# Three double banks in turn, one-hot products on GpSimd, and index arithmetic in single steps, in a kernel of attention and expert layers

## The chip, the cores and the metric

The kernel runs on one core of one Trainium2 chip. The metric is the time of one execution on the device in microseconds (us), lower is better; the median of several runs is quoted. Every experiment was timed in alternating rounds with the kernel before on the same chip. Experiments sent together share one chip, and the results number it (6, 9, 11 or 15); the chip of the first comparison was not recorded. Each number below names its chip.

Engines in the profiles: PE is the matmul engine (PEld its weight loads), DVE the vector engine, ACT the scalar engine, POOL is GpSimd (which here also issues nearly all transfers), SP issues the stores of the attention rows. "L526" is line 526 of the kernel; lines after the change are numbered 8 to 22 higher than the same lines before. A half-clock stretch is a stretch in which the recorded PE clock was 0.5.

## The reference

```python
# attention: q, k, v are (8 batches, 8 heads, 576 tokens, 64), k and v are averaged over groups of 8 tokens (72 left)
scores = (1/8) * q @ k_p^T ;  attn = softmax(scores) ;  o = attn @ v_p
x = o as 4608 tokens x 512
# expert layer: each token goes through the two layers of one of 8 experts (domain_id)
for e in range(8):
    mask = domain_id == e
    out[mask] = relu(x[mask] @ w1[e]) @ w2[e]      # w1: 512 x 1024, w2: 1024 x 512
```

## The kernel before

The work is a list of units with times in "slots", sorted and then issued in that order. The batches are taken in four pairs (pair 0 to 3). A slot is one score unit (two matmuls, then the exponential on ACT); 16 slots make a pair. Between them stand the mixing units (`av_unit`: eight matmuls, then reciprocal and product on DVE into `x_sb`), the pooling of keys and values, and the transposes of q. The rows of a token's expert are found by one-hot matmuls (`perm_*`) and some chains of short DVE operations. Rows are stored to `x_lin` in DRAM, gathered back by expert, transposed, and sent through the two expert layers. For experts 0 and 1, the first three blocks of rows come from pairs 0 to 2 alone ("early"); the other two ("late") need pair 3.

On-chip accumulator memory (PSUM) is shared by tags: `big` has two double banks, `wide` one double bank, `small` two single banks.

```python
turns = {"pre": ("big", "big", "wide"), "out": ("small", "small", "wide")}
def rot(kind):                       # rot2() takes from "pre", rot1() from "out"
    i = count_[kind]; count_[kind] = i + 1
    tag = turns[kind][i % 3]
    return {"big": big, "wide": wide, "small": small}[tag]()
# ... cut ...
def val(i):                          # product of the one-hots; two per pair
    nc.vector.tensor_tensor(box["vc"][:, i], box["eq"][:], thl[...].to_broadcast(...), op=ALU.mult)
# ... cut ...
def sc_unit(pr, bh):
    p = big()
    # two matmuls, then ACT: exp -> at
def av_unit(pr, cc):
    pv = wide() if pr < NP - 1 or cc < 4 else rot2()...
    # eight matmuls, DVE: reciprocal, then x_sb = pv * rcp; every third unit stores x_sb to x_lin
# ... cut ...
for i, (k0, k1) in enumerate(((2.0, 3.8), (4.0, 5.8), (6.0, 8.0), (18.0, 25.0))):
    put(perm_units(i), k0, k1)
    put([lambda i=i: perm_mm(i)], k1 + 0.7, k1 + 0.7)
put([perm_finish], 40.0, 40.0)       # 9 DVE steps in one block
put([orig_finish], 43.0, 43.0)       # 9 DVE steps
put([count], 46.0, 46.0)             # 12 DVE steps and a matmul
# ... cut ...
put([lambda i=i: run(turn_units_(0, i)) for i in range(2)], 62.0, 64.0)   # transposes, expert 0, early
put([lambda i=i: e0_unit(i) for i in range(8)], 64.2, 71.4)               # first layer, expert 0, early
run([x[2] for x in sorted(plan)])
# after the plan: the rest of experts 0 and 1
for e in range(2):
    for j in range(3, NBL):
        gather(e, j)                 # the late rows: wait for pair 3's stores
run(wload_units(2, 0, 1))            # 1 MB: first-layer weights of expert 2
run(merge(l2_units(0, 0, EARLY, e0["hT"]), turn_units(1, 0, 3)))
run(l1_units(1, 0, EARLY, he, 0))
run(wload_units(2, 1, 1))            # 1 MB: second-layer weights of expert 2
run(turn_units(0, 3, NBL))           # transposes of expert 0's late rows
# ... late parts of experts 0 and 1, gathers and transposes of expert 2, then experts 2 to 7 in one loop
```

The softmax here doesn't subtract the row's maximum and nothing guards it: scores larger than these inputs give would overflow.

## Time and profile before

| | |
|---|---|
| timed runs, first comparison | 274.4 us (273.3 to 275.0, 4 runs) |
| the profiled execution | 265.7 us (span 263.7 us) |

The profiled execution is 9 us shorter than the timed runs.

From the page of the kernel before: the span in 40 equal slices of 6.6 us, the busy share of PE in tenths, PE's clock and the busy share of the transfer engines.

```profile
PE   1785998998966867998889999999999999999990
...
PEclk9999599999995775799999999999999999999999
DMA  6999999999999934955994999989979969922022
```

The last row holds digits near 9 up to slice 14 (0 to 92 us): transfers run full through the attention. From slice 22 on PE holds 9: the experts are bound by matmuls. Between lies the part that can be shortened, slices 3 to 21.

The same execution by windows. Columns: window, its length, busy us (count) of PE, PEld, DVE, ACT, POOL, then PE's clock, the share of the transfer engines, GB/s.

```profile
70.00:80.00 10.00, 6.92 (x97) 4.81 (x95) 9.23 (x37) 5.25 (x8) 0.00 (x0) 0.92 1.03 244
80.00:90.00 10.00, 8.09 (x91) 5.62 (x92) 4.77 (x12) 4.99 (x9) 0.00 (x0) 0.56 1.16 245
90.00:100.00 10.00, 6.20 (x79) 3.99 (x76) 3.97 (x10) 6.71 (x13) 2.96 (x3) 0.78 0.54 163
100.00:110.00 10.00, 8.60 (x76) 5.41 (x75) 4.96 (x12) 2.12 (x4) 4.13 (x5) 0.54 0.66 121
110.00:120.00 10.00, 9.11 (x57) 4.93 (x56) 2.87 (x5) 3.05 (x6) 2.49 (x3) 1.00 0.61 147
130.00:140.00 10.00, 9.13 (x72) 6.51 (x70) 3.81 (x8) 2.74 (x7) 6.54 (x7) 1.00 1.11 281
```

From 70 to 80 us DVE is full (9.23 of 10) and PE is not (6.92). Then the clock is 0.54 to 0.78 for 30 us. What PE waited for, in total, times, longest:

```profile
PE wide L504 <- DVE x_sb L510: 5.0, 8, 0.7
PE turn L576 <- DMA xg<-x_lin,xrow: 2.2, 2, 1.3
PE small L364 <- DVE vc L352: 2.0, 1, 2.0
...
PE small L269 <- DVE nov L267: 1.1, 1, 1.1
...
PE big L597 <- DMA xg<-x_lin,xrow: 0.9, 1, 0.9
```

`x_sb` is the release of the single mixing bank; PE waited 5.0 us itself, and its weight loads 7.4 us. `vc` is the product of the one-hots, `nov` belongs to the count.

### The profile page before, as it was taken

Reading aid. Unit: us, or ns where it says so; the run is one execution under the profiler, and the core shown is the slowest. Engines: PE = TensorE matmul, PEld = TensorE weight load, DVE = VectorE, ACT = ScalarE, POOL = GpSimd, SP = SyncE. Lnnn points to the kernel's source line nnn. Section 1 sums busy time; section 2 is a strip of 40 time slices with the busy share of each in tenths; the row PEclk is TensorE's granted clock in tenths of the full one; section 3 lists DMA queues with packets and bytes.
Section 4 is the critical chain, followed back from the end, with each engine's and each line's share of the span. In section 5 each row is a group of like instructions: output and inputs, shape, how many; then the busy total and the mean of one; then the engine's idle time right before and its main releaser. Section 6 shows DMA issues by size and latency. Waiting matters only on the chain.

```text
span 263.7 us, 4980 instructions
## 1 busy us (share of the span) xinstructions
PE 230.8 (88%) x2048; PEld 148.1 (56%) x2048; DVE 124.4 (47%) x284; ACT 93.4 (35%) x157; POOL 101.3 (38%) x116
## 2 busy tenths in 40 slices
PE   1785998998966867998889999999999999999990
PEld 0664666676643644555566665665755755756640
DVE  7257788786785353524234334334234332343320
ACT  1045547877654671422132220230411312302210
POOL 7000000300000037027764775656655665734042
PEclk9999599999995775799999999999999999999999
DMA  6999999999999934955994999989979969922022
GB/s 113 207 218 218 210 221 224 239 240 241 247 243 245 241 106 157 140 145 107 243 236 162 165 237 250 221 240 205 240 187 204 259 122 211 268 109 98 2 101 92
DMA packets 18153, 50.19 MB, mean 190 GB/s; under 512 B 2316, under 2 KB 10574, under 8 KB 15568
## 3 DMA queue, kind: packets, MB, share of 16 engines
q0 software_dynamic: 16320, 45.10, 78.8%
q1 hardware_dynamic: 1808, 4.76, 4.9%
q8 instruction: 16, 0.26, 0.4%
q14 instruction: 9, 0.07, 0.1%
HBM read 67.15 MB, written 15.20 MB: 312 GB/s over the span
## 4 chain that ended last, share of the span: by engine, by line
PE 56%; DVE 14%; DMA 10%; issue 10%; POOL 4%; ACT 3%; POOLq 1%; DVEq 0%
PE big L597 13%; PE small L613 10%; PE wide L597 6%; PE wide L613 5%; DMA x_lin<-x_sb 4%; DMA out_dram<-y,tok 4%; POOL out_dram L622 4%; PE big L484 4%; DVE x_sb L510 3%; PE wide L504 3%; PE small L442 3%; PE small L413 3%; PE small L470 2%; DMA xg<-x_lin,xrow 2%; PE turn L576 2%
## 5 line engine op out<-in xcount | busy, mean ns | idle before, releaser
L562 POOL DMA_INDIRECT xg<-x_lin,xrow x40 | 40.6, 1016 | 72.3 <-DVE x_sb L510 45.3
L622 POOL DMA_INDIRECT out_dram<-y,tok x40 | 40.1, 1003 | 44.4 <-ACT y L620 20.7
L487 ACT ACTIVATE at<-big 72x576 f16<-72x576 f32 x64 | 40.2, 644 | 30.6 <-PE big L484 29.3
L613 PEld LDWEIGHTS <-hT 128*128 128x128 f16 x272 | 25.8, 98 | 26.7
L597 PEld LDWEIGHTS <-w 128*128 128x128 f16 x256 | 25.1, 100 | 13.9 <-issue 2.3
L603 DVE TENSOR_SCALAR hT<-big 128x640 f16<-128x640 f32 (+1 forms) x22 | 15.7, 716 | 33.1 <-PE big L597 33.1
L597 PE MATMUL big<-xT,w 128*128 128x320 f16 (+2 forms) x176 | 29.4, 312 | 1.8 <-DMA xg<-x_lin,xrow 0.9
L620 ACT ACTIVATE y<-small 128x512 f32<-128x512 f32 x14 | 8.4, 597 | 45.0 <-PE small L613 42.1
L601 ACT ACTIVATE hT<-big 128x640 f16<-128x640 f32 (+1 forms) x21 | 13.2, 627 | 29.0 <-PE big L597 29.0
L510 DVE TENSOR_TENSOR x_sb<-wide,rcp 128x512 f16<-128x512 f32 x33 | 22.8, 692 | 1.1
L484 PE MATMUL big<-qT,kpT 64*72 64x288 f16 x128 | 21.3, 338 | 2.0 <-DVE qT L474 1.9
L504 PE MATMUL wide<-vp,at 72*128 72x65 f16 (+1 forms) x288 | 16.8, 208 | 5.4 <-DVE x_sb L510 5.0
L577 DVE COPY xT<-turn 128x1024 f16<-128x1024 f16 (+1 forms) x24 | 14.3, 598 | 14.9 <-PE turn L576 14.9
L504 PEld LDWEIGHTS <-at 72*128 72x128 f16 (+1 forms) x320 | 14.7, 112 | 11.5 <-DVE x_sb L510 7.4
L613 PE MATMUL small<-w,hT 128*128 128x512 f16 x80 | 18.7, 379 | 0.0
L618 DVE COPY y<-small 128x512 f32<-128x512 f32 x13 | 9.0, 692 | 20.5 <-PE small L613 19.6
L576 PE MATMUL turn<-ident,xg 128*128 128x128 f16 x160 | 13.7, 226 | 2.2 <-DMA xg<-x_lin,xrow 2.2
L576 PEld LDWEIGHTS <-xg 128*128 128x128 f16 x160 | 11.1, 100 | 7.9 <-DMA xg<-x_lin,xrow 3.0
L597 PEld LDWEIGHTS <-k 128*128 128x128 f16 x128 | 12.5, 98 | 5.2
L508 DVE RECIPROCAL rcp<-wide 128x8 f32<-128x8 f32 x33 | 6.8, 205 | 16.3 <-PE wide L504 16.1
L597 PE MATMUL wide<-xT,w 128*128 128x320 f16 (+2 forms) x80 | 13.3, 299 | 0.8 <-DVE xT L577 0.8
L603 DVE TENSOR_SCALAR hT<-wide 128x640 f16<-128x640 f32 (+1 forms) x10 | 7.5, 745 | 13.3 <-PE wide L597 10.1
(158 smaller groups left out, 321.1 us busy)
## 6 DMA issues: line engine op xcount, KB each, us to landing
w<-in_moe_w_dram POOLq DMA_DIRECT2D x8, 1024.0 KB, 11.8
k<-in_k_dram POOLq DMA_DIRECT2D x4, 1152.0 KB, 27.9
q<-in_q_dram POOLq DMA_DIRECT2D x4, 1152.0 KB, 28.1
v<-in_v_dram POOLq DMA_DIRECT2D x4, 1152.0 KB, 25.3
x_lin<-x_sb SPq DMA_DIRECT2D x12, 384.0 KB, 10.3
k<-in_moe_w_dram POOLq DMA_DIRECT2D x3, 1024.0 KB, 8.5
v<-in_moe_w_dram POOLq DMA_DIRECT2D x3, 1024.0 KB, 11.0
q<-in_moe_w_dram POOLq DMA_DIRECT2D x2, 1024.0 KB, 11.2
```

The source lines that it names most:

```text
L484: nc.tensor.matmul(p[0:72, par, 0:288], s["kpT"][64 * par:64 * par + 64, bh, :], s["qT"][64 * par:64 * par + 64, :, 8 * bh:8 * bh + 8], st ...
L487: nc.scalar.activation(at[0:72, bh % 8, :].rearrange("p (a c) -> p a c", a=2), p[0:72, :, 0:288], AFT.Exp, scale=1.0 / 64.0)
L504: nc.tensor.matmul(pv[r0:r0 + z - a, h, 0:65], s["at", bt][0:72, h, a:z], s["vp"][0:72, 8 * bt + h, :], start=True, stop=True, skip_group_ ...
L510: nc.vector.tensor_tensor(out=x_sb.rearrange("p (b h a) -> p b h a", b=4, h=H), in0=pv[:, :, 0:64].rearrange("p h (a b) -> p b h a", b=4), ...
L562: i = nc.gpsimd.indirect_dma_start(out=xg[e % 2][:, j, :], out_offset=None, in_=x_lin[0:rows, :], in_offset=bass.IndirectOffsetOnAxis(ap=x ...
L576: nc.tensor.transpose(p[:, j - a, kk, :], xg[e % 2][:, j, 128 * kk:128 * kk + 128], ident[:])
L577: nc.vector.tensor_copy(xts[e][:, :, 128 * a:128 * z].rearrange("p k (j c) -> p j k c", c=128), p[:, 0:z - a])
L597: nc.tensor.matmul(p[:, a, 0:m], w1[:, kk, 128 * fi:128 * fi + 128], xT[:, kk, s0 + m * a:s0 + m * a + m], start=(kk == 0), stop=(kk == 3))
L601: nc.scalar.activation(dst, p[:, 0:nh, 0:m], AFT.Relu)
L603: nc.vector.tensor_scalar(out=dst, in0=p[:, 0:nh, 0:m], scalar1=0.0, scalar2=None, op0=ALU.max)
L613: nc.tensor.matmul(p, hT[:, fi, 128 * j:128 * j + 128], w2[:, fi, :], start=(fi == 0), stop=(fi == 7))
L622: i = nc.gpsimd.indirect_dma_start(out=out, out_offset=bass.IndirectOffsetOnAxis(ap=orig[0][:, bl:bl + 1], axis=0), in_=y[:], in_offset=No ...
```

## The change

The intent is to keep PE busy and warm from 20 to 110 us: scores and mixing rotate over three double banks instead of having two and one; the products go to idle GpSimd; the three DVE blocks are cut into single steps spread over slots 34 to 58, and the count moves behind the attention; pair 3's value pooling and the early expert work start 2 to 3 slots earlier; one 1 MB weight load goes behind the first gathers; the first expert units are reordered. The operations and their number are the same but for a few.

```diff
-                nc.vector.tensor_tensor(box["vc"][:, i], box["eq"][:],
+                nc.gpsimd.tensor_tensor(box["vc"][:, i], box["eq"][:],
@@ sc_unit
-            p = big()
+            p = rot2()
@@ av_unit
-            pv = wide() if pr < NP - 1 or cc < 4 else rot2().rearrange(...)
+            pv = rot2().rearrange(...)
@@ the plan
-                    at[4:] = [16.1, 17.4, 18.8, 20.2, 21.6]
+                    at[4:] = [16.1, 17.1, 18.2, 19.3, 20.4]
-                at = [9.2, 10.7, 12.2, 13.7, 16.1, 16.8, 17.5, 18.2, 18.9]
+                at = [9.2, 10.7, 12.2, 13.7, 16.1, 17.0, 17.9, 18.8, 19.7]
-            k0, k1 = (2.6, 6.6) if pr < NP - 1 else (3.6, 8.4)
+            k0, k1 = (2.6, 6.6) if pr < NP - 1 else (0.5, 6.5)
-        ... ((2.0, 3.8), (4.0, 5.8), (6.0, 8.0), (18.0, 25.0)) ... k1 + 0.7
+        ... ((2.0, 5.0), (5.0, 9.0), (9.0, 14.5), (18.0, 30.0)) ... k1 + 2.3
-        put([perm_finish], 40.0, 40.0)
-        put([orig_finish], 43.0, 43.0)
-        put([count], 46.0, 46.0)
+        put(perm_finish(), 34.0, 44.0)       # now a list of single steps
+        put(orig_finish(), 49.0, 58.0)
-        put(wload_units(1, 0, 1), 26.0, 26.0)
-        put([lambda j=j: gather(0, j, XE) for j in range(3)], 55.0, 58.0)
+        put([lambda j=j: gather(0, j, XE) for j in range(3)], 54.0, 57.0)
+        put(wload_units(1, 0, 1), 57.1, 57.1)
-        put([lambda i=i: run(turn_units_(0, i)) for i in range(2)], 62.0, 64.0)
+        put([lambda i=i: run(turn_units_(0, i)) for i in range(2)], 59.5, 61.5)
-        put([lambda i=i: e0_unit(i) for i in range(8)], 64.2, 71.4)
+        put([lambda i=i: e0_unit(i) for i in range(8)], 62.0, 69.6)
@@ after the plan
-        nblk = nc.values_load(nblk_i[0:1, 0:1], ...)          # moved down
-        run(merge(l2_units(0, 0, EARLY, e0["hT"]), turn_units(1, 0, 3)))
+        run([u[0], t[0], u[1], t[1], u[2]])
-        run(l1_units(1, 0, EARLY, he, 0))
+        run(merge(l1_units(1, 0, EARLY, he, 0), count_a() + [count_mm]))
         run(wload_units(2, 1, 1))
-        run(turn_units(0, 3, NBL))
+        run([v[0]] + turn_units(0, 3, NBL) + [v[1]])
-        run(merge(merge(u, l2_units(1, 0, EARLY, he)), [lambda j=j: gather(2, j) for j in range(NBL)]))
-        run(turn_units(1, 3, NBL))
+        run(merge(u[:5], g[:3] + count_b()) + [v[2]] + turn_units(1, 3, NBL) + merge(u[5:], g[3:]))
+        nblk = nc.values_load(nblk_i[0:1, 0:1], ...)
```

More of the change, by code (lines that the diff above doesn't have):

```diff
@@ L96, in small16, with __init__, __getattr__ @@
         return ps.tile([128, 8, 128], F16, tag="small", bufs=2, name="small16")
+    class Later:
+        def __init__(self):
+            self.units = []
+        def __getattr__(self, name):
+            return lambda *a, **kw: self.units.append(lambda: getattr(nc.vector, name)(*a, **kw))
     x_lin = dram.tile([XROWS, HD], F16, name="x_lin")
@@ L126 @@
         meta = const.tile([128, NCH, 2], I32, name="meta")
-        row_i = rt.tile([128, NCH], I32, name="row_i")
+        row_i = const.tile([128, NCH], I32, name="row_i")
         nc.gpsimd.iota(row_i[:], pattern=[[128, NCH]], base=0, channel_multiplier=1)
@@ L145 @@
                                 op0=ALU.is_gt)
-        ones = rt.tile([128, 128], F16, name="ones")
+        ones = const.tile([128, 128], F16, name="ones")
         nc.vector.memset(ones[:], 1.0)
@@ L249, in slot_post @@
             nonlocal od, slot_i
-            od = rt.tile([128, NCH], F32, name="od")
+            od = const.tile([128, NCH], F32, name="od")
             nc.vector.tensor_scalar(out=od[:], in0=ork[:, 0:NCH], scalar1=float(NBLK * 128),
@@ L258, in slot_post, with count_a @@
             nc.vector.tensor_copy(slot_i[:], od[:])
-        def count():
-            nonlocal mrow, mt, nblk_f, nblk_i, nov, nov_f, novp, ovs
-            nov = rt.tile([128, 2], F16, name="nov")
-            ovs = rt.tile([128, 1], F32, name="ovs")
-            nc.vector.tensor_reduce(out=ovs[:], in_=ovf[:], op=ALU.add, axis=AX.X)
-            nc.vector.tensor_copy(nov[:, 0:1], ovs[:])
-            nc.vector.tensor_copy(nov[:, 1:2], ovs[:])
-            novp = small()
+        def count_a():
+            nonlocal nov, ovs
+            v = Later()
+            nov = const.tile([128, 2], F16, name="nov")
+            ovs = const.tile([128, 1], F32, name="ovs")
+            v.tensor_reduce(out=ovs[:], in_=ovf[:], op=ALU.add, axis=AX.X)
+            v.tensor_copy(nov[:, 0:1], ovs[:])
+            v.tensor_copy(nov[:, 1:2], ovs[:])
+            return v.units
@@ L269, in count, with count_mm, count_b @@
+        def count_mm():
+            nonlocal novp
+            novp = rot1()
             nc.tensor.matmul(novp[:, 0:2], ones[:], nov[:], start=True, stop=True)
+        def count_b():
+            nonlocal mrow, mt, nblk_f, nblk_i, nov_f
+            v = Later()
             nov_f = const.tile([128, 1], F32, name="nov_f")
-            nc.vector.tensor_copy(nov_f[:], novp[:, 0:1])
+            v.tensor_copy(nov_f[:], novp[:, 0:1])
             nblk_f = const.tile([128, 1], F32, name="nblk_f")
-            nc.vector.tensor_scalar(out=nblk_f[:], in0=nov_f[:], scalar1=127.0, scalar2=None, op0=ALU.add)
+            v.tensor_scalar(out=nblk_f[:], in0=nov_f[:], scalar1=127.0, scalar2=None, op0=ALU.add)
@@ L274, in count @@
             nblk_i = const.tile([128, 1], I32, name="nblk_i")
-            nc.vector.tensor_copy(nblk_i[:], nblk_f[:])
-            nc.vector.tensor_scalar(out=nblk_i[:], in0=nblk_i[:], scalar1=7, scalar2=None,
+            v.tensor_copy(nblk_i[:], nblk_f[:])
+            v.tensor_scalar(out=nblk_i[:], in0=nblk_i[:], scalar1=7, scalar2=None,
                                     op0=ALU.logical_shift_right)
             mrow = const.tile([128, NCH], I32, name="mrow")
-            mt = rt.tile([128, NCH], F32, name="mt")
@@ L281, in count @@
-            nc.vector.tensor_scalar(out=mt[:], in0=ovf[:], scalar1=-float(BIG), scalar2=float(BIG - NBLK * 128),
+            mt = const.tile([128, NCH], F32, name="mt")
+            v.tensor_scalar(out=mt[:], in0=ovf[:], scalar1=-float(BIG), scalar2=float(BIG - NBLK * 128),
                                     op0=ALU.mult, op1=ALU.add)
-            nc.vector.tensor_tensor(mt[:], mt[:], od[:], op=ALU.add)
-            nc.vector.tensor_copy(mrow[:], mt[:])
-            nc.vector.tensor_copy(meta[:, :, 0], row_i[:])
@@ L286, in count @@
-            nc.vector.tensor_copy(meta[:, :, 1], dom[:])
+            v.tensor_tensor(mt[:], mt[:], od[:], op=ALU.add)
+            v.tensor_copy(mrow[:], mt[:])
+            v.tensor_copy(meta[:, :, 0], row_i[:])
+            v.tensor_copy(meta[:, :, 1], dom[:])
+            return v.units
         def perm_prep():
@@ L300, in perm_prep, with token_of @@
             nc.vector.tensor_copy(blk_h[:], blk_i[:])
-        def token_of(pool, row, n):
+        def token_of(pool, row, n, v=nc.vector):
             w = [pool.tile([128, n], I32, name="tok%d" % i) for i in range(6)]
             m, g, a, b, t, u = [i[:] for i in w]
-            nc.vector.tensor_scalar(out=m, in0=row, scalar1=3, scalar2=None, op0=ALU.logical_shift_right)
-            nc.vector.tensor_scalar(out=g, in0=row, scalar1=7, scalar2=None, op0=ALU.bitwise_and)
-            nc.vector.tensor_scalar(out=t, in0=m, scalar1=1821.0, scalar2=None, op0=ALU.mult)
-            nc.vector.tensor_scalar(out=a, in0=t, scalar1=16, scalar2=None, op0=ALU.logical_shift_right)
-            nc.vector.tensor_scalar(out=b, in0=a, scalar1=1, scalar2=None, op0=ALU.logical_shift_right)
-            nc.vector.tensor_scalar(out=t, in0=m, scalar1=2.0, scalar2=None, op0=ALU.mult)
-            nc.vector.scalar_tensor_tensor(out=u, in0=g, scalar=72.0, in1=t, op0=ALU.mult, op1=ALU.add)
-            nc.vector.scalar_tensor_tensor(out=t, in0=b, scalar=574.0, in1=u, op0=ALU.mult, op1=ALU.add)
-            nc.vector.scalar_tensor_tensor(out=u, in0=a, scalar=-71.0, in1=t, op0=ALU.mult, op1=ALU.add)
+            v.tensor_scalar(out=m, in0=row, scalar1=3, scalar2=None, op0=ALU.logical_shift_right)
+            v.tensor_scalar(out=g, in0=row, scalar1=7, scalar2=None, op0=ALU.bitwise_and)
+            v.tensor_scalar(out=t, in0=m, scalar1=1821.0, scalar2=None, op0=ALU.mult)
+            v.tensor_scalar(out=a, in0=t, scalar1=16, scalar2=None, op0=ALU.logical_shift_right)
+            v.tensor_scalar(out=b, in0=a, scalar1=1, scalar2=None, op0=ALU.logical_shift_right)
+            v.tensor_scalar(out=t, in0=m, scalar1=2.0, scalar2=None, op0=ALU.mult)
+            v.scalar_tensor_tensor(out=u, in0=g, scalar=72.0, in1=t, op0=ALU.mult, op1=ALU.add)
+            v.scalar_tensor_tensor(out=t, in0=b, scalar=574.0, in1=u, op0=ALU.mult, op1=ALU.add)
+            v.scalar_tensor_tensor(out=u, in0=a, scalar=-71.0, in1=t, op0=ALU.mult, op1=ALU.add)
@@ L315, in token_of, with row_of @@
             return w[5]
-        def row_of(pool, c, p, n):
+        def row_of(pool, c, p, n, v=nc.vector):
             w = [pool.tile([128, n], F32, name="row%d" % i) for i in range(2)]
             t, x = w[0][:], w[1][:]
-            nc.vector.tensor_scalar(out=t, in0=p, scalar1=float(LC - EC), scalar2=float(XE - EC),
+            v.tensor_scalar(out=t, in0=p, scalar1=float(LC - EC), scalar2=float(XE - EC),
                                     op0=ALU.mult, op1=ALU.add)
-            nc.vector.scalar_tensor_tensor(out=t, in0=c, scalar=float(EC), in1=t, op0=ALU.is_ge, op1=ALU.mult)
-            nc.vector.scalar_tensor_tensor(out=x, in0=p, scalar=float(EC), in1=t, op0=ALU.mult, op1=ALU.add)
-            nc.vector.tensor_tensor(x, x, c, op=ALU.add)
+            v.scalar_tensor_tensor(out=t, in0=c, scalar=float(EC), in1=t, op0=ALU.is_ge, op1=ALU.mult)
+            v.scalar_tensor_tensor(out=x, in0=p, scalar=float(EC), in1=t, op0=ALU.mult, op1=ALU.add)
+            v.tensor_tensor(x, x, c, op=ALU.add)
@@ L376, in perm_finish @@
         def perm_finish():
+            v = Later()
             cf = rt.tile([128, NBLK], F32, name="cf")
-            nc.vector.tensor_scalar(out=cf[:], in0=o_sum[:, 0:NBLK], scalar1=-1.0, scalar2=None, op0=ALU.add)
+            v.tensor_scalar(out=cf[:], in0=o_sum[:, 0:NBLK], scalar1=-1.0, scalar2=None, op0=ALU.add)
             em = rt.tile([128, NBLK], F32, name="em")
-            nc.vector.tensor_scalar(out=em[:], in0=cf[:], scalar1=0.0, scalar2=float(BIG),
+            v.tensor_scalar(out=em[:], in0=cf[:], scalar1=0.0, scalar2=float(BIG),
                                     op0=ALU.is_lt, op1=ALU.mult)
-            x = row_of(rt, cf[:], o_sum[:, NBLK:2 * NBLK], NBLK)
-            nc.vector.tensor_tensor(xrow[:], x[:], em[:], op=ALU.add)
-            nc.vector.scalar_tensor_tensor(out=cf[:], in0=cf[:], scalar=128.0, in1=em[:],
+            x = row_of(rt, cf[:], o_sum[:, NBLK:2 * NBLK], NBLK, v)
+            v.tensor_tensor(xrow[:], x[:], em[:], op=ALU.add)
+            v.scalar_tensor_tensor(out=cf[:], in0=cf[:], scalar=128.0, in1=em[:],
                                            op0=ALU.mult, op1=ALU.add)
-            nc.vector.tensor_tensor(crow[:], cf[:], o_sum[:, NBLK:2 * NBLK], op=ALU.add)
+            v.tensor_tensor(crow[:], cf[:], o_sum[:, NBLK:2 * NBLK], op=ALU.add)
+            return v.units
         def orig_finish():
-            orig.append(token_of(const, crow[:], NBLK))
+            v = Later()
+            orig.append(token_of(const, crow[:], NBLK, v))
+            return v.units
         st = {}
@@ L494, in av_unit @@
             x_sb = s["x"][:, cc % 3, :]
-            pv = wide() if pr < NP - 1 or cc < 4 else rot2().rearrange("p a (b c) -> p (a b) c", c=128)
+            pv = rot2().rearrange("p a (b c) -> p (a b) c", c=128)
             lo, hi = 128 * cc, 128 * cc + 128
@@ L678 @@
         put([perm_prep], 1.5, 1.5)
-        for i, (k0, k1) in enumerate(((2.0, 3.8), (4.0, 5.8), (6.0, 8.0), (18.0, 25.0))):
+        for i, (k0, k1) in enumerate(((2.0, 5.0), (5.0, 9.0), (9.0, 14.5), (18.0, 30.0))):
             put(perm_units(i), k0, k1)
-            put([lambda i=i: perm_mm(i)], k1 + 0.7, k1 + 0.7)
-        put([perm_finish], 40.0, 40.0)
-        put([orig_finish], 43.0, 43.0)
-        put([count], 46.0, 46.0)
+            put([lambda i=i: perm_mm(i)], k1 + 2.3, k1 + 2.3)
+        put(perm_finish(), 34.0, 44.0)
+        put(orig_finish(), 49.0, 58.0)
         for pr in range(2, NP):
@@ L709 @@
         late = main.enter_context(tc.tile_pool(name="late", bufs=3))
-        nblk = nc.values_load(nblk_i[0:1, 0:1], min_val=0, max_val=N // 128)
         for e in range(2):
@@ L715 @@
         run(wload_units(2, 0, 1))
-        run(merge(l2_units(0, 0, EARLY, e0["hT"]), turn_units(1, 0, 3)))
+        u = l2_units(0, 0, EARLY, e0["hT"])
+        t = turn_units(1, 0, 3)
+        run([u[0], t[0], u[1], t[1], u[2]])
         he = late.tile([128, 8, EARLY], F16, tag="hTl", bufs=1, name="hTe1")
-        run(l1_units(1, 0, EARLY, he, 0))
+        run(merge(l1_units(1, 0, EARLY, he, 0), count_a() + [count_mm]))
         run(wload_units(2, 1, 1))
-        run(turn_units(0, 3, NBL))
+        v = l2_units(1, 0, EARLY, he)
+        run([v[0]] + turn_units(0, 3, NBL) + [v[1]])
         h0 = hidden()
         u = l1_units(0, EARLY, CAP, h0, 0)
-        run(merge(merge(u, l2_units(1, 0, EARLY, he)), [lambda j=j: gather(2, j) for j in range(NBL)]))
-        run(turn_units(1, 3, NBL))
+        g = [lambda j=j: gather(2, j) for j in range(NBL)]
+        run(merge(u[:5], g[:3] + count_b()) + [v[2]] + turn_units(1, 3, NBL) + merge(u[5:], g[3:]))
+        nblk = nc.values_load(nblk_i[0:1, 0:1], min_val=0, max_val=N // 128)
         h1 = hidden()
```

## The prediction

> **What bounds the kernel now.** By windows of 10 us over the profiled execution (span 263.7 us): from 140 to 250 us PE is 100% busy at full clock (expert matmuls); this stays. From 20 to 110 us (attention) PE is the longest engine but not full: 7.3, 9.7, 8.9, 9.8, 8.9, 6.9, 8.1, 6.2, 8.6 us of each 10. A plan slot (one score unit) takes 1.09 us when all goes well: slots 16 to 32 took 17.5 us (timeline of PE, 41.6 to 59.0). Pairs 0, 2 and 3 took 21.1, 21.6 and about 22 us. The extra time:
> - 23.4 to 34 us: one-hot and product steps fill DVE (per pair op 1.5, eq 0.5, vc 1.0 us); PE waits 2.0 us for vc; the granted clock falls (0.86, 0.80).
> - 68 to 80 us: DVE is busy 9.2 of 10 us. Row chain (9 steps, 1.7 us), token chain (9 steps, 1.6 us) and count (12 steps, 2.0 us) run as blocks; PE waits 0.9, 0.5, 1.1, 1.1 us.
> - Then the clock is granted at 0.56, 0.78, 0.54 (80 to 110 us). Eight mixing matmuls take 0.62 us instead of 0.43, two score matmuls 0.46 instead of 0.31, four early-expert matmuls 1.46 instead of 0.81. The Trainium skill, "TensorE: Matmul & The Clock Gate", section on the HAM clock gate, says low PE activity halves the clock; this trace agrees in order: the idle at 74 to 80 us comes first.
> - Mixing has one double bank: PE or its weight load waits for x_sb about 0.65 us per unit at 82 to 98 us (waits: 5.0 and 7.4 us in all).
>
> **What the change does.** It moves eight products (0.49 us each) from DVE to GpSimd; estimate there about 1 us each (the Trainium skill, "GPSIMD Engine Reference", section 3: two-input work about 2 times slower), on an idle engine. It spreads the chains, moves count behind attention, gives scores and mixing three double banks in turn, starts pair 3's value pooling 3 slots earlier and early-expert transposes and matmuls 2.2 to 2.5 slots earlier, delays one 1 MB weight load behind the first gathers, and reorders the first expert units.
>
> **Worth, on the critical path.** Pair 0: -2 us. Pair 2: -3 us. Pair 3 up to the first transpose of gathered rows (99.5 us now): -3.5 us, mostly clock. From there to the late part of expert 0 (126.2 us): cold matmuls and three waits (1.3, 0.9, 0.8 us), -4 us. Given back: k and q of pair 3 land about 64 and 70 us (issue plus 28 us), 2 to 3 us before use, and the DMA share is 1.0 from 10 to 90 us, so attention can't run much faster; the chain last mixing unit, store (5.1 us), gather (1.1 plus about 2.5 us), transpose now meets PE earlier: a 1 to 3 us wait stays. Net about -12 us. Timed runs lie 9 to 11 us above the profile; I keep that offset.
>
> **Predicted: 262.5 us, 8 in 10 within 256 to 268.5. Faster by over 2%: 0.85; within: 0.13; slower: 0.02.**
>
> **Right if:** the granted clock stays near 1.0 from 70 to 110 us; slots 32 to 48 take about 18 us; PE waits for x_sb fall under 3 us; first transpose of gathered rows at 90 to 92 us; expert stage unchanged; span about 252 us. Wrong steps would show as PE waits for pair 3's loads, a wait over 3 us for gathered rows, or score matmuls waiting for x_sb.
>
> **What would make it wrong.** The clock still falls (a stall at the earlier transposes or at v of pair 3): then only 3 to 5 us are gained. Shared banks couple scores to a late DVE. If timed runs exceed the profile because they are colder, the gain is larger.

## The result, and the profile after

| | before | after | ratio (95% interval) |
|---|---|---|---|
| first comparison, chip not recorded | 274.4 us | 266.9 us (265.7 to 267.6) | 0.9726 (0.9676 to 0.9776) |
| both kernels again, chip 6 | 265.5 us | 261.8 us (261.6 to 262.8) | 0.9877 (0.9840 to 0.9914) |

A ratio is the mean time of one kernel's fast runs over that of the other's of the same rounds, so it is not quite the ratio of the medians.

The change is faster, by 7.5 us in the first comparison and by 3.7 us on chip 6. The predicted time, 262.5 us, was 4.4 us too low, and the range held it. But the profile of after, taken among its own timed runs (266.5 us), has a span of 264.7 us, while that of before had 263.7 us. The profile of before fits an execution on one of the faster chips: on chips 6, 9 and 11 the same kernel takes 265.5, 265.9 and 266.1 us, on chip 15 270.7 us. So those two profiles don't show a gain, and for comparison stage by stage both kernels were run again on chip 6 (labels e1_before and e2_after). The profile of before shown above agrees with e1_before to 1.3 us at every stage, so the lines above can be read against those of e2_after.

The page of after, from the first comparison's chip:

```profile
PE   1778889999777289998779989999999999999990
...
PEclk9997999999999558999979999999999999999997
DMA  6999999999999689819975999979989889722022
```

The clock row has one dip instead of a long one, and a hole stands in PE's row at slice 14 (digit 2, 86 to 93 us), with a second, flatter one at slices 20 and 21 (digits 7, 126 to 139 us), where the clock dips too. The same windows on chip 6 (e2_after):

```profile
70.00:80.00 10.00, 7.75 (x127) 5.85 (x128) 6.58 (x15) 5.84 (x10) 0.00 (x0) 1.00 1.03 243
80.00:90.00 10.00, 5.82 (x81) 3.93 (x77) 4.80 (x18) 7.51 (x15) 0.81 (x1) 0.82 1.02 236
90.00:100.00 10.00, 7.12 (x57) 4.00 (x58) 2.67 (x6) 2.82 (x5) 7.02 (x8) 0.50 0.74 140
100.00:110.00 10.00, 9.98 (x92) 6.09 (x89) 5.79 (x12) 3.04 (x7) 0.00 (x0) 0.99 1.08 259
110.00:120.00 10.00, 10.00 (x63) 5.56 (x61) 4.26 (x10) 3.06 (x6) 5.62 (x6) 1.00 0.28 64
130.00:140.00 10.00, 6.62 (x41) 3.61 (x39) 2.23 (x4) 0.99 (x3) 5.02 (x6) 0.88 0.95 243
```

What PE waited for in that execution (total, times, longest):

```profile
PE turn L598 <- DMA xg<-x_lin,xrow: 8.4, 3, 4.3
...
PE small L492 <- DMA q<-in_q_dram: 2.3, 2, 1.8
...
PE big L526 <- ACT at L509: 1.2, 3, 0.7
```

Windows 70:80 and 100:110 are what was wanted: the clock is 1.00 and 0.99 where it was 0.92 and 0.54 (0.83 and 0.63 in e1_before, on the same chip). The waits of PE for `x_sb`, `vc` and `nov` have left the list (its weight loads still wait 0.5 us for `x_sb`). In their place stand the gathered rows, 8.4 us in three waits. Window 130:140 is worse than before: PE busy 6.62 instead of 9.13.

Stages on chip 6, in us from the span's start, read from the timelines of PE (expert n starts with its first-layer matmuls):

| | pair 0 ends | pair 2 ends | first transpose of gathered rows | expert 1, early, first layer | expert 2 | expert 3 | expert 7 | last matmul |
|---|---|---|---|---|---|---|---|---|
| before | 41.7 | 79.5 | 99.8 | 119.1 | 147.5 | 166.0 | 239.7 | 257.2 |
| after | 39.8 | 75.7 | 92.2 | 111.6 | 144.4 | 162.8 | 236.6 | 254.1 |
| difference | -1.9 | -3.8 | -7.6 | -7.5 | -3.1 | -3.2 | -3.1 | -3.1 |

The column of the first transpose needs care: the change moves the transposes 2.5 slots forward in the plan, so 20 matmuls (two score units, two mixing units) that ran before them now run after them. At expert 1 the work done is the same again.

So 7.5 us are gained by the time expert 1 starts, and 4.4 us are given back before expert 2. The two stretches by their windows, with the same work in both kernels but for a few matmuls at the borders:

| | before: length, PE busy, PE idle | after |
|---|---|---|
| end of pair 2 to expert 1 | 39.6, 32.4, 7.2 | 35.9, 28.2, 7.7 |
| expert 1 to expert 2 | 28.4, 26.7, 1.7 | 32.8, 28.6, 4.2 |

In the first stretch PE has 4.2 us less to do for the same matmuls, because 24.4 us of it were at half clock before and 13.7 us after. Its idle time is no smaller: waits for `x_sb` were exchanged for waits for gathered rows. In the second stretch PE idles 2.5 us more and works 1.9 us longer. There it is, in the timeline of PE on chip 6 after the change (start, duration, what; in brackets the idle time before and what ended it):

```profile
130.98 1.89 PE L635 MATMUL small<-w,hT 128*128 128x512 f16 x8
136.25 0.75 PE L598 MATMUL turn<-ident,xg 128*128 128x128 f16 x8 [3.38 <-DMA xg<-x_lin,xrow]
136.84 2.78 PE L635 MATMUL wide<-w,hT 128*128 128x512 f16 x8
...
144.36 1.93 PE L619 MATMUL big<-xT,k 128*128 128x320 f16 x13
```

PE stands still from 132.9 to 136.25 for the rows of expert 2, and the next second-layer unit takes 2.78 us instead of 1.89: the clock is half from 137.7 to 141.1 us. Before the change the same transposes came without a wait:

```profile
139.50 1.89 PE L613 MATMUL small<-w,hT 128*128 128x512 f16 x8
141.22 0.61 PE L576 MATMUL turn<-ident,xg 128*128 128x128 f16 x8
141.67 1.89 PE L613 MATMUL small<-w,hT 128*128 128x512 f16 x8
```

Why the rows are late stands in the timeline of GpSimd, which issues gathers (DMA_INDIRECT) and weight loads (DMA_DIRECT2D) into one queue; expert 2's weights go to the buffers of k and v, whence the names:

```profile
113.16 1.05 POOL L584 DMA_INDIRECT xg<-x_lin,xrow  x1 [14.61 <-DMA x_lin<-x_sb]
...
118.16 0.61 POOL L578 DMA_DIRECT2D k<-in_moe_w_dram  x1
...
122.69 0.99 POOL L578 DMA_DIRECT2D v<-in_moe_w_dram  x1
...
126.60 1.06 POOL L584 DMA_INDIRECT xg<-x_lin,xrow  x1 [0.30 <-issue]
```

GpSimd waits 14.6 us for the stores of pair 3, then issues the late rows, 2 MB of weights, and the rows of expert 2. Before the change the first gather of late rows was issued at 117.5 us, 4.3 us later, about as much as the last mixing unit came later (108.9 against 104.3). So this chain of transfers moved by 4.3 us. But PE comes to the transposes of expert 2 at 132.9 instead of 141.2 us, 8.3 us earlier. Before the change PE came to them 13.0 us after the first gather for expert 2 was issued (at 128.25 us); now it comes 6.3 us after it (at 126.60), and has the rows only after 9.7 us. The landing times of that gather (`prof LABEL --tile xg`, a window on this one issue) close the account: 11.3 us from issue to landing before, so the rows were there at 139.5 us, 1.7 us before PE came; 9.6 us after the change, so they are there at 136.2 us. PE came 8.3 us earlier and the rows 3.3 us; less the 1.7 us of slack, that is the wait of 3.4 us. (This gather was issued only 1.7 us earlier, since GpSimd now issues five stores of results ahead of it instead of three.)

All this is chip 6. The profile of after from the first comparison's chip has the wait at the first transposes (4.2 us) but none for the rows of expert 2; there the stretch from expert 1 to expert 2 takes 33.3 us, with other waits (see e3_after_load). What was lost on that chip is not shown, since no profile of before comes from it.

### The profile page after: what moved, and what is told of

It reads as the page before. It is cut to its first block, busy times and chain, and to the rows that moved or that the text cites. A ratio compares the mean times of both kernels' runs of the same rounds, so it can differ in the third digit from the quotient of the medians.

```text
span 264.7 us, 4980 instructions
## 1 busy us (share of the span) xinstructions
PE 228.1 (86%) x2048; PEld 144.7 (55%) x2048; DVE 121.0 (46%) x276; ACT 93.0 (35%) x157; POOL 108.4 (41%) x124
## 4 chain that ended last, share of the span: by engine, by line
PE 55%; DMA 22%; issue 9%; POOL 5%; DVE 4%; ACT 2%; POOLq 1%; DVEq 0%
DMA v<-in_v_dram 19%; PE big L619 18%; PE small L635 13%; PE wide L619 8%; PE wide L635 6%; POOL out_dram L644 3%; PE turn L598 3%; PE small L464 3%; DMA x_lin<-x_sb 2%; PE big L506 2%; DVE x_sb L532 1%; PE big L526 1%; ACT hT L623 1%; DMA xg<-x_lin,xrow 1%; DVE qT L496 1%
## 5 line engine op out<-in xcount | busy, mean ns | idle before, releaser
L509 ACT ACTIVATE at<-big 72x576 f16<-72x576 f32 x44 | 28.2, 645 | 21.0 <-PE big L506 14.2
L623 ACT ACTIVATE hT<-big 128x640 f16<-128x640 f32 (+1 forms) x21 | 13.2, 627 | 34.7 <-PE big L619 27.3
L635 PE MATMUL small<-w,hT 128*128 128x512 f16 x72 | 18.1, 394 | 0.4 <-ACT hT L623 0.4
L598 PE MATMUL turn<-ident,xg 128*128 128x128 f16 x160 | 13.7, 226 | 5.0 <-DMA xg<-x_lin,xrow 5.0
L526 PEld LDWEIGHTS <-at 72*128 72x128 f16 (+1 forms) x320 | 13.9, 105 | 5.3 <-issue 1.5
L506 PE MATMUL big<-qT,kpT 64*72 64x288 f16 x88 | 14.5, 324 | 2.1 <-DVE qT L496 1.7
L625 DVE TENSOR_SCALAR hT<-wide 128x640 f16<-128x640 f32 (+1 forms) x11 | 7.9, 714 | 18.4 <-PE wide L619 11.8
L532 DVE TENSOR_TENSOR x_sb<-big,rcp 128x512 f16<-128x512 f32 x23 | 15.9, 691 | 0.8
L619 PE MATMUL wide<-xT,w 128*128 128x320 f16 (+2 forms) x84 | 14.4, 305 | 1.8 <-DVE hT L625 0.9
L509 ACT ACTIVATE at<-wide 72x576 f16<-72x576 f32 x20 | 12.9, 645 | 5.2 <-PE wide L506 5.0
L492 PE MATMUL small<-ident,q 128*128 128x128 f16 x144 | 10.7, 219 | 3.9 <-DMA q<-in_q_dram 2.5
```

The source lines that it names most:

```text
L506: nc.tensor.matmul(p[0:72, par, 0:288], s["kpT"][64 * par:64 * par + 64, bh, :], s["qT"][64 * par:64 * par + 64, :, 8 * bh:8 * bh + 8], st ...
L509: nc.scalar.activation(at[0:72, bh % 8, :].rearrange("p (a c) -> p a c", a=2), p[0:72, :, 0:288], AFT.Exp, scale=1.0 / 64.0)
L526: nc.tensor.matmul(pv[r0:r0 + z - a, h, 0:65], s["at", bt][0:72, h, a:z], s["vp"][0:72, 8 * bt + h, :], start=True, stop=True, skip_group_ ...
L532: nc.vector.tensor_tensor(out=x_sb.rearrange("p (b h a) -> p b h a", b=4, h=H), in0=pv[:, :, 0:64].rearrange("p h (a b) -> p b h a", b=4), ...
L598: nc.tensor.transpose(p[:, j - a, kk, :], xg[e % 2][:, j, 128 * kk:128 * kk + 128], ident[:])
L619: nc.tensor.matmul(p[:, a, 0:m], w1[:, kk, 128 * fi:128 * fi + 128], xT[:, kk, s0 + m * a:s0 + m * a + m], start=(kk == 0), stop=(kk == 3))
```

## The experiments

Where the texts use letters, L is the theory that the late load of a register (`values_load`, now in the middle of expert work) costs the lost time, and D the theory that the order and time of transfers do. Every kernel below computed the reference's result. Ratios are against the kernel before on the same chip. Places in time of runs on chips 9 and 11 are compared below with those of e2_after on chip 6; these three chips agree on the time of before within 0.6 us and on an expert (18.4 us), but each place is read from one profile.

| label | what | ratio | 95% interval | chip |
|---|---|---|---|---|
| e1_before | before | 1.0022 | 0.9978 to 1.0066 | 6 |
| e2_after | after | 0.9877 | 0.9840 to 0.9914 | 6 |
| e3_after_load | after, register load later | 0.9874 | 0.9833 to 0.9915 | 6 |
| e4_banks | before, banks in turn | 1.0141 | 1.0105 to 1.0176 | 6 |
| e5_after_w2 | after, one weight load later | 0.9951 | 0.9904 to 0.9999 | 9 |
| e6_banks_phase | e4 with the expert banks as before | 0.9939 | 0.9897 to 0.9981 | 9 |
| e7_products_dve | after, products on DVE | 0.9806 | 0.9744 to 0.9869 | 9 |
| e8_blocks | after, row and token steps as blocks | 0.9894 | 0.9844 to 0.9944 | 9 |
| e9_after_early | after, two weight loads earlier | 0.9867 | 0.9808 to 0.9925 | 11 |
| e10_early_turn | e9, early expert work back in its old place | 0.9922 | 0.9861 to 0.9984 | 11 |
| e11_before_early | before, the same loads earlier | 1.0184 | 1.0120 to 1.0249 | 11 |
| e12_split | after, one of the two loads earlier | 1.0000 | 0.9952 to 1.0048 | 15 |

### e1_before and e2_after: both kernels on one chip

No edit. These two exist to have both profiles on the same chip.

> The kernel before, unchanged, for a profile beside its timed runs (the first profile, 265.7 us, was 8 to 9 us faster than all its timed runs). Ratio 1.00. If the timed runs are the typical ones, this profile has a span near 272 us. Theory A (clock): the added 8 us lie between 70 and 130 us as a longer stretch of half clock. Theory B (PE slower in the expert stage): the added time lies after 140 us, spread over the experts.

> The changed kernel again, ratio 0.973 as measured. In its first profile PE finished the last two or three first-layer units of each expert about 1.46 us apart instead of 1.09. If that belongs to the kernel, it is here again at the same places; if it belongs to that execution or chip, it is elsewhere, or in the kernel before too.

Measured: 265.7 and 261.8 us; the stages are in the table above. The gain is 1.2% here against 2.7% in the first comparison.

### e3_after_load: the register load moved

In the profile of after on the first comparison's chip the loss between 126 and 139 us looked different. There PE waits four times for ACT and DVE, which lag after the register load, and not for rows:

```profile
129.25 0.60 PE L619 MATMUL big<-xT,w 128*128 128x256 f16 x4
130.66 0.60 PE L619 MATMUL big<-xT,w 128*128 128x256 f16 x4 [0.81 <-ACT hT L623]
132.15 0.60 PE L619 MATMUL wide<-xT,w 128*128 128x256 f16 x4 [0.90 <-DVE hT L625]
133.53 0.60 PE L619 MATMUL big<-xT,w 128*128 128x256 f16 x4 [0.78 <-ACT hT L623]
134.99 0.98 PE L619 MATMUL big<-xT,w 128*128 128x256 f16 x4 [0.86 <-DVE hT L625]
...
136.61 2.81 PE L635 MATMUL small<-w,hT 128*128 128x512 f16 x8
```

So the first theory was the register load.

```diff
-        nblk = nc.values_load(...)
         h1 = hidden()
         run(l1_units(1, EARLY, CAP, h1, 0))
         u = l2_units(0, EARLY, CAP, h0) + l2_units(1, EARLY, CAP, h1)
-        run([u[0], wload_units(3, 0, 1)[0], t[0], ...])
+        run([u[0]])
+        nblk = nc.values_load(...)
+        run([wload_units(3, 0, 1)[0], t[0], ...])
```

> The changed kernel with the register load of the block count moved four matmul groups later, behind the first second-layer unit of expert 0's late part. Theory L (the load stalls ACT and DVE about 2.5 us each while first-layer units come every 0.44 us, PE runs dry at 129 to 136 us and the clock halves for 3.4 us): 4 to 5 us faster than the changed kernel, ratio to before about 0.957. Rival (the slow stretch at 129 to 136 us is the slow PE of that execution): no change against the changed kernel, 0.973.

Measured: 262.1 us against 261.8 of after on the same chip; expert 2 starts at 144.4 us in both. But the run does not test the theory where it arose: on chip 6 ACT and DVE do not lag there in e2_after either (from 127 to 132 us ACT is idle at most 0.7 us before one of its steps and DVE 0.5 us, against 2.5 us on the first chip), so there was nothing to gain. On chip 6 the loss before expert 2 is the wait for rows, and not the register load. Whether the load makes the lag on the first chip stays open.

### e4_banks: only the banks in turn, in the kernel before

```diff
-            p = big()
+            p = rot2()
-            pv = wide() if pr < NP - 1 or cc < 4 else rot2().rearrange(...)
+            pv = rot2().rearrange(...)
```

> The kernel before with only the three double banks in turn for scores and mixing. If waits for x_sb (5.0 and 7.4 us before) and the half clock that follows are what the change removes: about 0.98. If the blocks of index arithmetic at 68 to 80 us are what matters: 0.99 to 1.00.

Measured: 1.4% slower. The attention ends 0.8 us earlier (mixing at 108.1), but three of the experts take 19.4 to 19.5 us instead of 18.4. Their waits:

```profile
PE wide L613 <- DVE hT L603: 0.9, 1, 0.9
PE wide L597 <- DVE y L618: 0.8, 1, 0.8
PE wide L597 <- ACT y L620: 0.7, 1, 0.7
```

A second-layer unit and the first-layer unit right after it land on the one bank `wide`, so PE waits for DVE or ACT to empty it. Two rotations, one for the first layer and one for the second, have this bank as their third place. The edit makes 95 more units draw from the first of them ahead of the experts (64 of scores, 31 of mixing); 95 leaves 2 when divided by 3, so the two rotations now meet on the bank.

### e6_banks_phase: the same, with the phase put back

```diff
@@ e4_banks, after the plan
+        count_["pre"] += 1
```

> The kernel before with the three double banks in turn, and the turn's counter set back so that the expert stage uses the same banks as before. If e4 lost its time (3.5 us) to a new collision of the two rotations on the shared bank in the expert stage (three experts of 19.4 us instead of 18.4), this is 0.99 to 1.00 of before, with every expert at 18.4 us. If sharing the banks itself costs time in attention, it stays at 1.01.

Measured: 0.9939, experts at 18.4 us again and no wait of PE listed from 145 to 250 us. So the loss of e4 was the collision, and the banks by themselves are worth about 0.6%. Pair 2 ends at 79.5 us as before, and half clock is granted from 76.5 to 86.7 and from 93.5 to 107.2 us: without the DVE part of the change the clock still falls. The waits for `x_sb` shrink, but those for gathered rows at the first transposes grow from 2.1 us (e1_before) to 4.7 us: here too PE comes earlier and the rows do not.

### e7_products_dve: the products back on DVE

```diff
-                nc.gpsimd.tensor_tensor(box["vc"][:, i], box["eq"][:],
+                nc.vector.tensor_tensor(box["vc"][:, i], box["eq"][:],
```

> The changed kernel with the eight products on DVE again. If moving them matters (4 us of DVE work in pairs 0 and 1): 1.5 to 2.5 us slower than the changed kernel up to slot 16. Rival (spreading alone is enough, as DVE has room once its work is not in blocks): within 0.5 us of the changed kernel.

Measured: 0.9806, not slower than after (0.9877 on another chip; the intervals overlap). Expert 2 starts at 144.5 and expert 3 at 162.9 us, as in after. One product takes (min/median/max ns) on GpSimd in after and on DVE here:

```profile
L370 POOL TENSOR_TENSOR vc<-eq,thl x8: 780/785/1092, 24.6 to 51.2; 128x360 f16<-128x360 f16 x8
```

```profile
L370 DVE TENSOR_TENSOR vc<-eq,thl x8: 522/524/533, 25.3 to 57.5; 128x360 f16<-128x360 f16 x8
```

The move to GpSimd works as such, but no wait for `vc` comes back without it: spreading the steps over more slots had already made room. In this profile pair 0 ends 0.5 us later than in e2_after and pair 2 1.5 us later (half clock lasts from 40.8 to 47.6 us), and PE then waits 4.5 us for the gathered rows. At expert 2 nothing is left of it, and no gain shows in the time.

### e8_blocks: row and token arithmetic as two blocks again

```diff
-        put(perm_finish(), 34.0, 44.0)
-        put(orig_finish(), 49.0, 58.0)
+        put([lambda: run(perm_finish())], 40.0, 40.0)
+        put([lambda: run(orig_finish())], 43.0, 43.0)
```

> The changed kernel with the row and token arithmetic as two blocks of 9 steps again (count stays behind attention). If blocks stall PE (0.5 to 1.1 us each in the kernel before) and the clock then falls: 2 to 4 us slower at the start of pair 3's scores, and a half clock near 75 us. Rival (the shared banks and the missing count already give slack): within 1 us.

Measured: 0.9894. Pair 2 ends at 78.3 and the mixing at 107.2 us, 2.6 and 2.9 us later than in e2_after, but expert 3 starts at 163.9, only 1.1 us later. Attention time again is worth less than itself at the end. The clock is half from 71.8 to 102.5 us; the profile shows a wait of 1.8 us for q of pair 3 just ahead of it, which e2_after has too without losing the clock at that place. The later start of pair 3 and the half clock near 75 us are what the first reading expected, but one profile can't tell whether the blocks or that wait brought the clock down.

```profile
70.00:80.00 10.00, 7.98 (x82) 6.05 (x82) 5.79 (x19) 4.14 (x6) 0.00 (x0) 0.59 1.02 240
80.00:90.00 10.00, 9.54 (x95) 6.83 (x96) 4.20 (x10) 5.52 (x11) 0.00 (x0) 0.50 1.03 237
```

### e5_after_w2: the second weight load of expert 2 behind its gathers

This tests D: the weights are what the rows of expert 2 stand behind.

```diff
-        run(wload_units(2, 1, 1))
         v = l2_units(1, 0, EARLY, he)
         ...
         run(merge(u[:5], g[:3] + count_b()) + [v[2]] + turn_units(1, 3, NBL) + merge(u[5:], g[3:]))
+        run(wload_units(2, 1, 1))
```

> The changed kernel with one move: the second weight load of expert 2 is issued after expert 2's row gathers instead of before them. Theory G (in both profiles' twin of the changed kernel PE waits 3.4 us at 133 to 136 us for gathered rows that lie behind 1 MB weight loads in the same queue, and the clock is halved for the next 3.4 us): the wait and the half clock vanish, the first unit of expert 2 starts at about 140 us instead of 144.4, and the kernel is 4 to 5 us faster than the changed one, ratio to before about 0.97 where the changed kernel has 0.988. Rival (the wait comes from the gathers' own issue order on GpSimd or from the register load): under 1 us.

Measured: expert 2 starts at 139.0 instead of 144.4 us, so the wait at expert 2 did come from the weights ahead of it in the queue. (GpSimd issues the first of these gathers 1.7 us earlier, at 124.86 us, and it lands 5.0 us after its issue instead of 9.6, so the earlier issue is the smaller part.) But expert 3 starts at 162.9, as in after:

```profile
149.44 1.89 PE L635 MATMUL small<-v,hT 128*128 128x512 f16 x8
155.16 1.03 PE L598 MATMUL turn<-ident,xg 128*128 128x128 f16 x8 [3.83 <-DMA xg<-x_lin,xrow]
155.99 2.92 PE L635 MATMUL small<-v,hT 128*128 128x512 f16 x8
```

The same wait, 3.8 us, stands one expert later, and half clock follows it again (154.6 to 158.1 us; the unit takes 2.92 instead of 1.89). The gain against before was smaller than that of after on its chip, and the runs scattered from 261.9 to 265.5 us; the profile is of the fastest, so what made the other three slower is not known.

### e9_after_early: both weight loads of expert 2 before the attention ends

The transfers have a hole in after: window 110:120 above moves 64 GB/s, because GpSimd stands waiting for pair 3's stores. The loads can go there.

```diff
         put(wload_units(1, 1, 1), 61.1, 61.1)
+        put(wload_units(2, 0, 1) + wload_units(2, 1, 1), 61.2, 61.3)
@@ after the plan
-        run(wload_units(2, 0, 1))
-        run(wload_units(2, 1, 1))
```

> The changed kernel with both weight loads of expert 2 issued about 15 us earlier, before GpSimd starts to wait for pair 3's stored rows. Theory D (the queue of transfers is the limit behind attention: its share is 0.28 at 110 to 120 us while GpSimd waits to issue, then gathers wait behind weights; four variants all start expert 3 at 162.8 to 162.9 us): the waits for gathered rows of experts 2 and 3 vanish, expert 3 starts at about 158 us, 3 to 5 us faster than the changed kernel, ratio to before 0.97 to 0.976. Rival (the transfers are limited by bytes in all, the gap at 110 us cannot be used): expert 3 stays at 162.8 us and the ratio at 0.985 to 0.99.

Measured: 0.9867, no better than after. The hole is filled (share 1.12 in window 110:120) and experts 2 and 3 don't wait, but now the late rows of expert 0 do. They are issued at 114.44 us, 1.3 us later than in e2_after, and stand behind the weights (the second of them lands 6.8 us after its issue, against 2.7 in e2_after):

```profile
116.83 1.89 PE L635 MATMUL small<-w,hTe 128*128 128x512 f16 x8
122.46 0.62 PE L598 MATMUL turn<-ident,xg 128*128 128x128 f16 x8 [3.74 <-DMA xg<-x_lin,xrow]
122.92 3.16 PE L635 MATMUL wide<-w,hTe 128*128 128x512 f16 x8
```

Expert 3 starts at 162.6 us.

### e10_early_turn: e9 with the early expert work in its old slots

```diff
-        put([lambda i=i: run(turn_units_(0, i)) for i in range(2)], 59.5, 61.5)
+        put([lambda i=i: run(turn_units_(0, i)) for i in range(2)], 62.0, 64.0)
-        put([lambda i=i: e0_unit(i) for i in range(8)], 62.0, 69.6)
+        put([lambda i=i: e0_unit(i) for i in range(8)], 64.2, 71.4)
```

> As e9, and the first expert's early transposes and matmuls at the places of the kernel before (2.2 to 2.5 slots later). In the changed kernel PE waits 4.2 us for the gathered rows at 88 to 92 us and the clock is halved for 13.6 us. If the earlier place only turns useful work into a wait: the wait falls under 2 us, the half clock is shorter, and it is 1 to 3 us faster than e9. If the earlier place is a gain: 1 to 2 us slower than e9.

Measured: 263.2 us against 262.0 of e9 on the same chip. The score units now end at 95.4 us (98.0 in e9), since PE doesn't stand before them, and expert 1 starts at 110.6 us, 1.0 us earlier than in e9: up to there the old slots are better. Behind the wait for the late rows of expert 0 (3.5 us, 3.7 in e9) half clock then lasts 10.2 us instead of 3.4, and expert 3 starts at 164.1, 1.5 us later. So the time favours the earlier slots by 1.2 us, but the loss arises elsewhere, and a gain of these slots as such is not shown. The wait for rows in attention fell to 1.7 and 1.5 us, but the half clock there (13.7 us) did not get shorter.

### e11_before_early: the same earlier loads in the kernel before

```diff
+        put(wload_units(2, 0, 1) + wload_units(2, 1, 1), 61.2, 61.3)
-        run(wload_units(2, 0, 1))
-        run(wload_units(2, 1, 1))
```

> The kernel before with the same earlier loads, as a control. Its expert stage never waited for transfers, so theory D expects no gain: 0.995 to 1.005. If the earlier loads help by themselves, it is faster by 2 us or more.

Measured: 271.0 us, 1.8% slower; I had expected no difference. PE waits three times for gathered rows, 5.3 us in all; two of these waits stand in e1_before too (2.1 us). The new one, 3.3 us, is for the late rows, and half clock follows it (127.7 to 134.5 us), so expert 2 starts at 153.6 instead of 147.5 us. The weights delay these rows twice. GpSimd issues the first late gather 3.5 us later (121.0 instead of 117.5), because the stores of pair 3 that it waits for land later; and this gather then lands 6.4 us after its issue instead of 2.8. So the place of a load sets the time here; its size was not varied.

### e12_split: one of the two loads earlier

```diff
+        put(wload_units(2, 0, 1), 61.2, 61.2)
@@ after the plan
-        run(wload_units(2, 0, 1))
+        run(wload_units(2, 1, 1))
         ...
-        run(wload_units(2, 1, 1))
```

> The changed kernel with expert 2's first weight load issued early (as in e9) and its second in the place where the first stood (ahead of the late rows of nobody, 4 us before expert 2's gathers). e5 moved the wait for gathered rows to expert 3, e9 moved it to the late rows of expert 0. Theory D (order and the idle stretch of the queue, not bytes, make the wait): with the 1 MB loads spread, no wait for gathered rows over 1 us after 100 us, expert 3 starts at about 158 us, ratio to before about 0.972. Rival (bytes: whatever the order, the queue is full until expert 3 and one wait of about 3.8 us comes back somewhere): ratio 0.985 to 0.99 again, expert 3 at 162.8 us.

Measured: 270.6 against 270.7 us of before, ratio 1.0000, on chip 15. PE still waits twice for late rows, 1.5 and 0.8 us, and before expert 2 it idles 4.1 us more in three gaps for which the profile shows no releaser; as this profile is slow, nothing is built on it. The fix that D promised did not come. The run stands beside before alone: after was not run on that chip, so how after does there is not known, and no version was shown to beat it (the 0.9806 of e7_products_dve overlaps with its 0.9877).

## Why the prediction was right or wrong

**The verdict and the range: right.** Faster by over 2% (0.85) came true in the first comparison, and 266.9 us lies in 256 to 268.5. The gain was predicted as 12 us and measured as 7.5 us. On chip 6 it is 3.7 us, and there the verdict would have been "within 2%". So the verdict holds in part by luck of the chip, and the range because it was wide. What the prediction itself named as its danger ("The clock still falls ...: then only 3 to 5 us are gained") fits chip 6 better than its main line; but there the lost clock is only part of the loss.

**Up to the first transpose of gathered rows: right in sum, not in each part.** Predicted -2 for pair 0, -3 for pair 2, -3.5 for pair 3, in all -8.5 us; measured on chip 6 -1.9, -1.4 (and -0.5 in pair 1) and -3.8, in all -7.6 us. Pair 2 gave half of what was predicted. Pair 3's -3.8 us was called "mostly clock"; it is the sum of 5.9 us less PE work and 2.1 us more idle time, and of the work about 2 us (an estimate: two score units of 0.46 and two mixing units of 0.62 us at half clock) was only moved behind the transposes. So its size is right partly by luck. The first transpose came at 92.2 us (predicted 90 to 92), the waits for `x_sb` fell to almost nothing (predicted under 3 us), slots 32 to 48 took 19.0 us (predicted about 18).

**"The granted clock stays near 1.0 from 70 to 110 us": half right.** It holds in windows 70:80 and 100:110. Between them half clock lasts 13.7 us (86.5 to 100.1). Before, it lasted 27.3 us in two stretches. The Trainium skill, "TensorE: Matmul & The Clock Gate", Part 1, gives an activity window of 3.41 us and, for the gate that follows PE's activity, only two rates, half and full; the stretches here agree, with lengths of 3.4, 6.8 and 13.7 us. The stretch in after starts at 86.5, before the long wait for rows: in the 3.4 us ahead of it PE was busy 2.31 us and waited twice for `at` (0.2 and 0.7 us). It lasts over the wait of 4.3 us that follows.

**"A 1 to 3 us wait stays": mis-sized.** It was 4.2 plus 0.8 us on the first chip, 4.3 plus 0.7 us on chip 6, past the 3 us that the prediction itself gave as the mark of a wrong step. It was also counted once, where on chip 6 it came at two places.

**"From there to the late part of expert 0: cold matmuls and three waits, -4 us": the step that failed.** From the first transpose to expert 1's early part it took 19.3 us before and 19.4 after on chip 6, with the 20 matmuls more that were moved here: the cold matmuls were not saved. The half clock after the transpose lasts 7.9 us (92.2 to 100.1) instead of 7.6. From expert 1 to expert 2, which the prediction took to be unchanged, it took 4.4 us longer: 2.5 us more idle (one wait of 3.4 us for rows of expert 2) and 1.9 us more work at half clock. The prediction listed PE's own waits and cold matmuls and removed them. It did not ask when the next transfers can be there. They hang on the last mixing unit, which came 4.6 us earlier, while PE came to the rows of expert 2 8.3 us earlier. The rows of expert 2 had only 1.7 us of slack before. So expert 2 starts only 3.1 us earlier, and everything after it is matmul-bound and keeps that.

That the order of the queue makes this wait is shown on chips 9 and 11: moving one load out of the way removes the wait at expert 2 (e5), moving two loads ahead of the late rows creates one there (e9, e11; in e11 half of the delay comes through the later stores). The Trainium skill, "DMA: Bandwidth & Descriptors", section "Two DMAs through the same engine are not ordered", says that within one queue of one DMA engine descriptors start in order; the rows that land late behind 1 and 2 MB of weights agree with that. Why e5 and e9, which move the wait to quite different places, both end within 0.3 us of after at expert 3 (162.9, 162.6, 162.8) is not settled. The profiles hint at a next bound close behind: PE starts the transposes of expert 3 at 156.5 us in e2_after and 156.3 in e9, without a wait, and at 155.2 in e5, where it has waited for the rows. So the rows left e5 only 1.3 us to gain there, and the half clock after the wait took that. A bound by the whole chain of transfers would do it, but no run removes both waits.

**"Timed runs lie 9 to 11 us above the profile; I keep that offset": failed.** A run's time lies only 1.8 to 2.0 us above its own span (266.5 and 264.7 for after, 264.9 and 263.0 for e1_before, 265.7 and 263.7 for the profile of before). The other 7 to 9 us lay between executions, not between a profile and its run; chips 6 and 15 differ by 5.2 us for the same kernel. On the first comparison's chip and on chip 15 an expert takes 19.1 and 19.0 us, on chips 6, 9 and 11 it takes 18.4, at a recorded clock of 1.00 in either case. For six experts that is 4 us. What causes it was not found, nor why the change gains 7.5 us on that chip and 3.7 us on chip 6; there is no profile of before from that chip.

**Where the parts stand.** Banks alone: 0.6% (e6), and a loss if their phase is left to chance (e4). Products on GpSimd: nothing (e7). Single steps instead of blocks: about 2.7 us of attention, about 1 us at the end, in one profile and not separated in the times (e8). Earlier expert work: 1.2 us in the time (e10 against e9), but not by its own effect as far as the profiles show. The moved count and the earlier value pooling were not tried alone.

## What to carry to other kernels

When a change lets the busiest engine arrive earlier, ask for each later input when its transfer can be issued and what stands ahead of it in the queue; gain beyond that point is given back, and at a clock that falls in the wait it is given back with interest. Two rotations that share one buffer must be checked against each other, since a change in the count of one shifts where they meet. Compare stage by stage only profiles from the same chip, and do it before trusting an offset between profile and timed runs.

## What the Trainium skill lacked or had wrong

- "TensorE: Matmul & The Clock Gate", Part 1, says that the clock falls after an idle window and returns after about 3.4 us of sustained work. In e8_blocks it stayed at half for 30.7 us, through 80 to 90 us with PE busy 9.54 of 10 us (as the profile counts it; the matmuls bear the half clock out, two score matmuls taking 0.46 instead of 0.31 us); in e2_after it fell after a window in which PE was busy 2.31 of 3.4 us. No page gives the share of a window that has to be busy.
- "GPSIMD Engine Reference", section 3.1, gives 1.96 times DVE's time for an addition of two inputs (fp32, 2048 elements). Here a product, 128x360 in fp16 with one broadcast input, took 785 against 524 ns, 1.5 times.
- "Perfetto Trace Analysis", section "Matmuls", advises to rotate matmul groups through different PSUM banks. It lacks the warning that two rotations sharing a bank can meet on it: 1.4% slower in e4_banks, 0.6% faster with the phase put back.
- No page has the difference between chips: the same kernel took 265.5 us on chip 6 and 270.7 us on chip 15, with experts of 18.4 against about 19 us at a recorded clock of 1.00.
